# One turn per token tile in the first two tiles of a two-stage mixer, and a later split of one weight piece

## The chip, the cores and the metric

The kernel runs on one core of one Trainium2 chip. The metric is the device time of one execution in microseconds (us); less is better. Times of single instructions and waits come from one profiled execution.

## The reference

The input `x` is eight batches of 4096 tokens with 192 channels, in float32. A causal convolution of seven taps, with softmax-normalised weights per head, gives the tokens `x` of the mixer:

```python
u  = x + (relu(x.T @ w_tok1) @ w_tok2).T      # mixing over tokens, 4096 -> 256 -> 4096
out = u + relu(u @ w_ch1) @ w_ch2             # mixing over channels, 192 -> 1536 -> 192
```

The weights `w_tok1`, `w_tok2`, `w_ch1` and `w_ch2` come as 64-bit floats. The kernel reads their two 32-bit words and rebuilds a 32-bit float from them ("decoding").

## The kernel before

The batches are worked in groups: 0, 1, then three pairs. A group has eight tiles of 512 tokens. For each tile the kernel makes `u` (`mix2`: a product with `w_tok2` and an addition), turns it (TensorE transposes, so that channels lie on partitions), multiplies by `w_ch1` (`channel1`, six steps p = 0 to 5, each making two blocks of 128 of the 1536 columns, "a pair"), and by `w_ch2` (`channel2`). Most operands are held as a high part, rounded to the matmul's format, and a low part, which is the rest: ScalarE (ACT) copies the high part out of PSUM and VectorE (DVE) subtracts it. So `own_hi` and `own_lo` are the parts of the turned tokens, and `hh` and `hl` those of relu's result `h`. A step p of `channel1` is 18 matmuls on half the array's rows, two by two: high by high, low weight by high, and high weight by low, for three chunks of 64 channels (`channel1_mm`, L1220). Six PSUM buffers `ps_x` are shared by all of this.

Group 0's tile 0 is made while the weights are still being decoded: `stage1_first` writes out by hand the order of decoding, convolution and the hooks of tile 0 (L670 to L772). Tile 0 works without splitting `h`, with `first_channel2`; tile 1 is the first that runs through `channel1`. In these two tiles `u` is held twice, side by side (`doubled`, L1033; ACT copies the second one, L1093), and `transposed` (L1130) turns three chunks of 128 columns, each of them one chunk of 64 channels in both halves of the partitions. All later tiles of groups 0 and 1 use `transposed_once` (L1146): two chunks of 128 columns hold all 192 channels, and ACT then moves halves of them to the other half of the partitions for the third chunk: two moves for `own_hi` at once, and two for `own_lo` in the returned function (L1159 to L1161).

The instructions of each engine stand in the order in which the program writes them, and each engine works them off in that order. A planner (`Background`) decides where the work of the next group, the "background", is written between: it keeps two counters of planned time, `pe` and `dve`. `fg(pe, dve, after)` is called with every piece of the foreground and adds to both; `fill(after)` then writes background items as long as `dve` is less than `pe + after` (L105). The convolution of group 1 is such a background: its first item (`tap`, L938, and `taps`, L839) needs the first half of a block of `x` in the tile `raw0`, loaded by SyncE's queue (SP, L807), with a small GpSimd (POOL) memset on it (L809). Its gate is planned time, 10,000 counts after the load was written (L936), not the landing itself.

After tile 0, `first_channel2(..., transposed)` turns tile 1 in the midst of tile 0's last product (L1564). `second_split` (L777) ends the decoding of the last piece of `w_tok2` that is needed early (`t_second`) and splits it into `t2s`. The tiles `hh0`, `hl0` and so on of tile 1 lie in memory that tile 0 and the decoding used until then (`ht_ctx.close()`, L1572).

Of the kernel before, what the change touches and what calls it, by code (L numbers as in the profile page):

```python
# [142 lines left out]
def conv_mixer_kernel(ctx: ExitStack, tc: tile.TileContext, x, weight, w_tok1, w_tok2, w_ch1, w_ch2, out):  # L143
# [299 lines left out]
    def stage1_first(pe, p0, p1, pd, late, load_u, after, pieces, hooks):  # L443
# [308 lines left out]
        begin(N1 + 3)  # L752
        woven(chains[N1 + 2][1:])
# [22 lines left out]

        def second_split():  # L777
            woven(chains[LAST2 + 1][2:])
            woven(split(LAST2 + 1))

        return second, second_split
# [243 lines left out]
    def load_tile(gi, q, pool):  # L1025
# [7 lines left out]
        doubled = gi == 0 and q < 2  # L1033
        u = up.tile([P, TJ, ND, 2 if nb > 1 or doubled else 1, D2], F32, name="u", bufs=2)
        for i in range(nb):
            at = u[:, :, :, 1 if doubled else i]
# [18 lines left out]
    def mix2(gi, q, t2, u, at_once=False, turned=None, between=()):  # L1055
# [15 lines left out]
        for j in range(TJ):  # L1071
# [16 lines left out]
            one, two = uj[:, :, uj.shape[2] - 1], uj[:, :, 0]  # L1088
            if at_once:
                if j < len(between):  # L1090
                    between[j]()
                nc.vector.tensor_tensor(out=two, in0=rows(ps[:, :D]), in1=one, op=ALU.add)
                nc.scalar.copy(out=one, in_=two)  # L1093
            elif nb == 1:
                nc.vector.tensor_tensor(out=one, in0=rows(ps[:, :D]), in1=one, op=ALU.add)
                nc.vector.tensor_tensor(out=two, in0=rows(ps[:, D:2 * D]), in1=one, op=ALU.add)
# [32 lines left out]

    def transposed(u, between=()):  # L1130


        own = own_tile("hi"), own_tile("lo")
        for c in range(ND):
            ps = ps_x.tile([P, TT], F32, name="ps_x")
            for j in range(TJ):
                cols = u[:, j, c].rearrange("p b d -> p (b d)")
                nc.tensor.transpose(out=ps[:, j * P:(j + 1) * P], in_=cols, identity=ident)
            bg.fg(440, 600)
            nc.scalar.copy(out=own[0][:, c], in_=ps)  # L1140
            nc.vector.tensor_tensor(out=own[1][:, c], in0=ps, in1=f32(own[0][:, c]), op=ALU.subtract)
            if c < len(between):
                between[c]()
        return [(own, own)]
# [54 lines left out]
    def first_u(tokens_mm):  # L1199
        first["u"] = None, up.tile([P, TJ, ND, 2, D2], F32, name="u", bufs=2)  # L1200
# [4 lines left out]
        def out():  # L1205
            for k, ps in enumerate(pss):
                nc.scalar.copy(
                    out=first["u"][1][:, 2 * k:2 * k + 2, :, 1],
# [8 lines left out]
    def first_transposed(between=()):  # L1217
        first["abc"] = transposed(first["u"][1], between)

    def channel1_mm(t, p, order=((0, 0), (1, 0), (0, 1))):  # L1220
# [41 lines left out]
    def channel1(t):  # L1262
        h = {}
        for f0 in range(0, NF, NF // 3):
            for n in ("hh", "hl"):
                part = hp.tile([P, NF // 3, TT], F32R, name=f"{n}{f0}")
                for f in range(NF // 3):
                    h[n, order[f0 + f]] = part[:, f]
        bg.tiled = True
        for p in range(NP):  # L1270
            pss = channel1_mm(t, p)
# [86 lines left out]
    second, second_split = stage1_first(  # L1358
# [19 lines left out]
    sp = None  # L1378

# [72 lines left out]
    for gi, bs in enumerate(GROUPS):  # L1452
# [13 lines left out]
        for q in range(NT):  # L1466
            nxt = (gi, q + 1) if q + 1 < NT else (gi + 1, 0)
            for i, b in enumerate(bs):
# [19 lines left out]
                if ahead:  # L1488
                    h = channel1(abc[i])
# [62 lines left out]
                else:  # L1552
# [56 lines left out]
```

## Time and profile before

| what | value |
|---|---|
| median of 3 runs | 2010.44 us (2009.76 to 2010.59) |
| the profiled execution's own time | 2009.58 us |
| its span, first to last instruction | 2007.8 us |
| TensorE (PE) busy | 1999.8 us, 100% |
| VectorE (DVE) busy | 1506.9 us, 75% |
| ScalarE (ACT) busy | 785.6 us, 39% |
| chain that ended last | PE 93%, DVE 3%, DMA 2%, ACT 1% |

The span leaves out what lies around the first and last instruction, 1.78 us here. A matmul's end is modelled, so that rows of PE overlap; the pitch of their starts tells the rate. In rows of the timeline the bracket gives the engine's idle time before the instruction and what ended it.

### The profile page before, as it was taken

Reading aid. Unit: us, or ns where it says so; the run is one execution under the profiler, and the core shown is the slowest. Engines: PE = TensorE matmul, PEld = TensorE weight load, DVE = VectorE, ACT = ScalarE, POOL = GpSimd, SP = SyncE. Lnnn points to the kernel's source line nnn. Section 1 sums busy time; section 2 is a strip of 40 time slices with the busy share of each in tenths; the row PEclk is TensorE's granted clock in tenths of the full one; section 3 lists DMA queues with packets and bytes.
Section 4 is the critical chain, followed back from the end, with each engine's and each line's share of the span. In section 5 each row is a group of like instructions: output and inputs, shape, how many; then the busy total and the mean of one; then the engine's idle time right before and its main releaser. Section 6 shows DMA issues by size and latency. Waiting matters only on the chain.

```text
span 2007.8 us, 45323 instructions
## 1 busy us (share of the span) xinstructions
PE 1999.8 (100%) x19007; PEld 1860.0 (93%) x19007; DVE 1506.9 (75%) x3022; ACT 785.6 (39%) x1308; POOL 212.2 (11%) x375
## 2 busy tenths in 40 slices
PE   9999999999999999999999999999999999999999
PEld 9899999999999999999999999999999999999998
DVE  6899989999559999757888789556666666666664
ACT  6677544444343343323333433333233322333322
POOL 1000000000011101111101110111111110011110
PEclk9999999999999999999999999999999999999999
DMA  9946455553354567515346544533323222333310
GB/s 305 307 150 219 137 166 171 181 180 136 123 158 124 142 176 205 156 58 140 86 127 190 140 128 115 137 88 85 86 64 81 71 65 64 82 86 85 85 48 17
DMA packets 281792, 259.26 MB, mean 129 GB/s; under 512 B 190084, under 2 KB 231620, under 8 KB 281588
## 3 DMA queue, kind: packets, MB, share of 16 engines
q1 hardware_dynamic: 258404, 172.85, 30.7%
q0 software_dynamic: 22656, 83.12, 13.7%
q8 instruction: 150, 2.46, 0.5%
q14 instruction: 54, 0.44, 0.1%
q10 hardware_dynamic: 528, 0.39, 0.1%
HBM read 147.25 MB, written 71.30 MB: 109 GB/s over the span
## 4 chain that ended last, share of the span: by engine, by line
PE 93%; DVE 3%; DMA 2%; ACT 1%; SPq 0%; issue 0%; POOL 0%; ACTq 0%; POOLq 0%; DVEq 0%
PE ps_x L1231 38%; PE ps_x L1292 26%; PE ps_x L1311 11%; PE ps_x L1312 5%; PE ps_x L1110 3%; PE ps_a L925 2%; PE ps_a L926 2%; PE ps_a L927 2%; PE ps_x L1080 1%; PE ps_a L921 1%; PE ps_x L1083 1%; DMA dec_raw<-in_moe_w_tok_dram 1%; DVE xc L819 1%; PE ps_x L1085 1%; PE ps_x L1084 1%; PE ps_x L1154 1%
## 5 line engine op out<-in xcount | busy, mean ns | idle before, releaser
L1274 ACT ACTIVATE hh<-ps_x 128x512 fp32r<-128x512 f32 x756 | 410.5, 596 | 827.5 <-PE ps_x L1231 827.4
L1275 DVE SCALAR_TENSOR_TENSOR hl<-ps_x,hh 128x512 fp32r<-128x512 f32 x756 | 483.9, 683 | 173.5 <-ACT hh L1274 172.8
L1292 PE MATMUL ps_x<-w,hh 64*128 64x384 f32 x3648 | 523.4, 355 | 0.0
L1292 PE MATMUL ps_x<-w,hl 64*128 64x192 f32 x3648 | 462.0, 247 | 0.0
L1231 PE MATMUL ps_x<-other,w_hi 64*128 64x512 f32 x1728 | 448.0, 387 | 0.3 <-ACT other L1190 0.2
L819 DVE SCALAR_TENSOR_TENSOR xc<-raw,cw,xc 128x384 f32<-128x384 f32 (+1 forms) x768 | 388.4, 559 | 9.2 <-ACT xc L817 9.1
L1292 PEld LDWEIGHTS ps_x<-w,hl 64*128 64x128 f32 x3648 | 357.1, 188 | 1.7 <-DVE hl L1275 0.3
L1292 PEld LDWEIGHTS ps_x<-w,hh 64*128 64x128 f32 x3648 | 351.0, 184 | 1.4
L1231 PE MATMUL ps_x<-own_hi,w_hi 64*128 64x512 f32 x1440 | 348.4, 392 | 1.6 <-ACT own_hi L1140 0.5
L1311 PE MATMUL ps_x<-w,hh 128*128 128x384 f32 x1200 | 348.1, 361 | 0.0
L1231 PEld LDWEIGHTS ps_x<-other,w_hi 64*128 64x128 f32 x1728 | 315.2, 184 | 31.2 <-ACT other L1190 0.5
L1231 PE MATMUL ps_x<-own_hi,w_lo 64*128 64x512 f32 x1440 | 342.4, 387 | 0.0
L1231 PE MATMUL ps_x<-own_lo,w_hi 64*128 64x512 f32 x1440 | 342.3, 386 | 0.0
L1312 PE MATMUL ps_x<-w,hl 128*128 128x192 f32 x1200 | 300.4, 250 | 0.0
L1231 PEld LDWEIGHTS ps_x<-own_hi,w_hi 64*128 64x128 f32 x1440 | 214.6, 184 | 30.9 <-issue 4.3
L1231 PE MATMUL ps_x<-other,w_lo 64*128 64x512 f32 x864 | 242.0, 386 | 0.0
L1231 PEld LDWEIGHTS ps_x<-own_lo,w_hi 64*128 64x128 f32 x1440 | 219.3, 184 | 24.2
L1231 PEld LDWEIGHTS ps_x<-own_hi,w_lo 64*128 64x128 f32 x1440 | 219.1, 184 | 24.3
L1312 PEld LDWEIGHTS ps_x<-w,hl 128*128 128x128 f32 x1200 | 229.1, 191 | 0.0
L1311 PEld LDWEIGHTS ps_x<-w,hh 128*128 128x128 f32 x1200 | 225.3, 188 | 0.5 <-DVE hl L1275 0.4
L1300 DVE TENSOR_TENSOR osb<-ps_x,osb 128x192 f32<-128x192 f32 x456 | 163.0, 357 | 26.8 <-PE ps_x L1110 0.5
L1231 PEld LDWEIGHTS ps_x<-other,w_lo 64*128 64x128 f32 x864 | 159.0, 184 | 16.1
(187 smaller groups left out, 2022.7 us busy)
## 6 DMA issues: line engine op xcount, KB each, us to landing
raw<-in_x_dram SPq DMA_DIRECT2D x56, 672.0 KB, 7.6
t<-t2d SPq DMA_DIRECT2D x64, 512.0 KB, 5.5
out_dram<-osb POOLq DMA_DIRECT2D x62, 384.0 KB, 4.2
xcd<-xc POOLq DMA_DIRECT2D x28, 768.0 KB, 7.8
u<-xcd SPq DMA_DIRECT2D x56, 384.0 KB, 5.7
t<-t1p SPq DMA_DIRECT2D x32, 512.0 KB, 5.8
other<-own_hi POOLq DMA_DIRECT2D x24, 384.0 KB, 3.9
other<-own_lo POOLq DMA_DIRECT2D x24, 384.0 KB, 4.0
```

The lines of the kernel that those rows point to most:

```text
L819: nc.vector.scalar_tensor_tensor(out=dst, in0=src, scalar=cw[:, h, k:k + 1], in1=dst, op0=ALU.mult, op1=ALU.add)
L925: nc.tensor.matmul(out=ps, lhsT=wh, rhs=xh, start=a, stop=False)
L926: nc.tensor.matmul(out=ps, lhsT=wh, rhs=xl, start=False, stop=False)
L927: nc.tensor.matmul(out=ps, lhsT=wl, rhs=xh, start=False, stop=z)
L1110: nc.tensor.matmul(out=ps[:, :n], lhsT=t2[ks, kc, r, j, :], rhs=h1[ks, kc, v, :n], start=m == 0, stop=m == len(prods) - 1)
L1231: nc.tensor.matmul(out=ps, lhsT=w1[w][rows, chunks[h][c], p * P:(p + 1) * P], rhs=t[h][v][rows, c], start=n == 0, stop=n == len(prods) - 1,)
L1274: nc.scalar.activation(out=h["hh", f], in_=ps, func=AF.Relu)
L1275: nc.vector.scalar_tensor_tensor(out=h["hl", f], in0=ps, scalar=0.0, in1=f32(h["hh", f]), op0=ALU.max, op1=ALU.subtract)
L1292: nc.tensor.matmul(out=ps[:, :m], lhsT=h[part, f][ks, ts], rhs=w2[ks, f, :m], start=n == 0 and part == "hh", stop=z and part == "hl",)
L1300: nc.vector.tensor_tensor(out=osb[:, j], in0=v, in1=osb[:, j], op=ALU.add)
L1311: nc.tensor.matmul(out=ps[:, :2 * D], lhsT=h["hh", f][:, ts], rhs=w2[:, f, :], start=n == 0, stop=False)
L1312: nc.tensor.matmul(out=ps[:, :D], lhsT=h["hl", f][:, ts], rhs=w2[:, f, :D], start=False, stop=z)
```

## The change

- **Tokens turned once.** `transposed` and `doubled` go; tiles 0 and 1 use `transposed_once`, with `u` held once. ACT no longer copies `u`. Tile 0's two moves of `own_lo` (`first["rest"]`) stand behind the start of the next decoding; tile 1's stand right behind `first_channel2`.
- **Order of the products.** Only in step p = 0 are the products of the third chunk put last; the other steps take chunk after chunk.
- **First parts of h in idle memory.** In tile 1, `channel1` puts `hh` and `hl` of the first two steps into the tiles `stage` and `xc1` of the background's pools (`early_parts`), all but the second low part.
- **The last piece of `w_tok2`.** Its decoding ends before tile 1's `channel1` (`second_end`); it is split (`second_split`) behind the second pair's `hh`.
- **Planner.** The extra counts on `dve` are 4000 and then 2000 in place of 6000, and the stores of `w_tok2` may begin after tile 1 in place of tile 0.

```diff
+        first["rest"]()                         # stage1_first, behind begin(N1 + 3)
...
+        def second_end():
+            woven(chains[LAST2 + 1][2:])
+
         def second_split():
-            woven(chains[LAST2 + 1][2:])
             woven(split(LAST2 + 1))
+            bg.dve = max(bg.dve, bg.pe) + 2e3
...
-        doubled = gi == 0 and q < 2
-        u = up.tile([P, TJ, ND, 2 if nb > 1 or doubled else 1, D2], F32, name="u", bufs=2)
+        u = up.tile([P, TJ, ND, nb, D2], F32, name="u", bufs=2)
...
-                nc.vector.tensor_tensor(out=two, in0=rows(ps[:, :D]), in1=one, op=ALU.add)
-                nc.scalar.copy(out=one, in_=two)
+                nc.vector.tensor_tensor(out=one, in0=rows(ps[:, :D]), in1=one, op=ALU.add)
...
+        if len(t) > 2 and not p:
             prods = [(w, v, c) for cs in (range(ND - 1), [ND - 1]) for w, v in order for c in cs]
...
+    def early_parts():
+        high, low = (td.tile([P, 2 * TT], F32R, name="stage", bufs=2).rearrange("p (f t) -> p f t", t=TT) for _ in range(2))
+        more = sp0.tile([P, NF // 4, TT], F32R, name="xc1")
+        return ("hh", 0, high), ("hl", 0, low), ("hh", 2, more)
...
             for f, ps in pss:
                 nc.scalar.activation(out=h["hh", f], in_=ps, func=AF.Relu)
+            if early and p == 1:
+                between()
+                part("hl", 0, range(2, 4))
+            for f, ps in pss:
...
-                    h = channel1(abc[i])
+                    h = channel1(abc[i], second_split, early_parts if gi == 0 and q == 1 else None)
...
-                        first_channel2(u, osb, [3], (NF // 3, lambda: made.extend(transposed(loaded[1]))))
-                        abc = made
-                        second_split()
-                        first["parted"] = 0.0
-                        bg.dve = max(bg.dve, bg.pe) + 6e3
+                        first_channel2(u, osb, [3], (NF // 3, lambda: made.extend(transposed_once(loaded[1]))))
+                        abc, rest = made
+                        rest()
+                        second_end()
+                        bg.dve = max(bg.dve, bg.pe) + 4e3
...
+                if gi == 0 and q == 1:
+                    first["parted"] = 0.0
```

The order of the instructions on ACT, from the turning of tile 1 to its first relu results; `own_hi` and `own_lo` are tile 1's turned tokens, `xc` is the convolution of group 1, `raw` its input, `hh` relu's high part. Before:

```order
L1140 CAST own_hi<-ps_x 128x512 x3
L240 CAST t2s<-t_second 128x2x512
L1325 DMA out_dram<-osb 128x4x192
L1274 ACTIVATE hh_929<-ps_x 128x512 x4
L1274 ACTIVATE hh_931<-ps_x 128x512 x4
L1274 ACTIVATE hh_933<-ps_x 128x512 x2
L199 ACTIVATE dec_top<-dec_raw 128x512
L817 ACTIVATE xc_1077<-raw_787,cw 128x8x24 x2
```

And with the change (its lines are numbered anew: L1142 is the copy of `own_hi`, L1146 and L1147 are the moves, L821 the first tap, L1269 relu, L1324 the store):

```order
L1142 CAST own_hi<-ps_x 128x512 x2
L1146 CAST own_hi<-own_hi 64x512
L1147 CAST own_hi<-own_hi 64x512
L821 ACTIVATE xc_896<-raw_780,cw 128x8x24 x2
L1146 CAST own_lo<-own_lo 64x512
L1147 CAST own_lo<-own_lo 64x512
L1324 DMA out_dram<-osb 128x4x192
L1269 ACTIVATE stage<-ps_x 128x512 x2
L1269 ACTIVATE xc_919<-ps_x 128x512 x2
L240 CAST t2s<-t_second 128x2x512
```

The first two taps of the convolution moved from behind ten relu copies to a place ahead of tile 1's moves of `own_lo`.

The matmuls of tile 1's step p = 0 on PE, behind the turning, and the first rows of p = 1, with the change; before, p = 0 had the form in which p = 1 stands here:

```order
L1140 MATMUL ps_x<-ident,u 128x128 x8
L1237 MATMUL ps_x<-w2f,t2s 128x192
L1237 MATMUL ps_x<-w2f,h_last 128x192 x3
L1218 MATMUL ps_x<-own_hi,w_hi 128x512 x4
L1218 MATMUL ps_x<-own_hi,w_lo 128x512 x4
L1218 MATMUL ps_x<-own_lo,w_hi 128x512 x4
L1218 MATMUL ps_x<-own_hi,w_hi 128x512 x2
L1218 MATMUL ps_x<-own_hi,w_lo 128x512 x2
L1218 MATMUL ps_x<-own_lo,w_hi 128x512 x2
L1218 MATMUL ps_x<-own_hi,w_hi 128x512 x6
```

The last two matmuls of p = 0 read the third chunk of `own_lo`, which ACT's two moves make. The turning is 8 transposes in place of 12.

The loads around `raw` on SP's queue, with the change; before, the same loads stood in the same order:

```order
L538 DMA xcd_75<-kept_x_119 90x8x192
L538 DMA xcd_75<-kept_x_119 32x8x192
L262 DMA dec_raw<-in_moe_w_tok_dram 128x1024 x2
L811 DMA raw_780<-in_x_dram 128x14x96
L811 DMA raw_783<-in_x_dram 128x14x96
L874 DMA t_786<-t1d 128x512
```

Nothing moved there: `raw_780`, which the first tap reads, is the third load after the stores `xcd` as before.

## Rows read from the trace of the kernel before

**Rows 1.** The page's chain that ended last, by engine.
```profile
PE 93%; DVE 3%; DMA 2%; ACT 1%; SPq 0%; issue 0%; POOL 0%; ACTq 0%; POOLq 0%; DVEq 0%
```

**Rows 2.** Waits of PE over the whole span: us in total, times, longest us.
```profile
PE ps_x L612 <- POOL ident masks.py:199: 1.4, 1, 1.4
```

**Rows 3.** Timeline of PE, tile 1: start us, us, engine, line, what.
```profile
87.32 1.47 PE L1138 MATMUL ps_x<-ident,u 128*128 128x128 f32 x12
88.63 0.49 PE L1250 MATMUL ps_x<-w2f,t2s 128*128 128x192 f32 x2
...
90.03 0.96 PE L1231 MATMUL ps_x<-own_hi,w_hi 64*128 64x512 f32 x6
...
94.92 0.84 PE L1231 MATMUL ps_x<-own_hi,w_lo 64*128 64x512 f32 x6
95.60 0.84 PE L1231 MATMUL ps_x<-own_lo,w_hi 64*128 64x512 f32 x6
96.67 1.56 PE L1231 MATMUL ps_x<-own_hi,w_hi 64*128 64x512 f32 x6 [0.23 <-DVE hl L1275]
...
102.62 1.06 PE L1231 MATMUL ps_x<-own_lo,w_hi 64*128 64x512 f32 x6
```

**Rows 4.** Timeline of ACT, the same stretch.
```profile
87.96 1.56 ACT L1140 CAST own_hi<-ps_x 128x512 fp32r<-128x512 f32 x3 [1.22 <-PE ps_x L1138]
93.71 1.05 ACT L240 CAST t2s<-t_second 128x1024 fp32r<-128x1024 f32 x1 [4.19 <-DVE t_second L208]
93.73 0.46 ACTq L1325 DMA_DIRECT2D out_dram<-osb  x1
94.66 3.03 ACT L1274 ACTIVATE hh<-ps_x 128x512 fp32r<-128x512 f32 x6
...
102.99 0.79 ACT L817 ACTIVATE xc<-raw,cw 128x192 f32<-128x192 f32 x2
```

**Rows 5.** Timeline of SP's queue: issues of DMAs.
```profile
70.01 4.19 SPq L1043 DMA_DIRECT2D u<-xcd  x4
...
88.76 1.65 SPq L262 DMA_DIRECT2D dec_raw<-in_moe_w_tok_dram  x2
90.51 3.28 SPq L807 DMA_DIRECT2D raw<-in_x_dram  x2
...
101.23 1.80 SPq L1043 DMA_DIRECT2D u<-xcd  x4
```

**Rows 6.** Instructions on the tile `raw`, 85 to 112 us: issue to landing.
```profile
DMA to landing us min/median/max: 8.3/9.6/11.0
```

**Rows 7.** Timeline of POOL, the memset on `raw`'s first half.
```profile
99.19 0.57 POOL L809 MEMSET raw<- 1x576 f32 x1 [87.19 <-DVE hl L1275]
```

**Rows 8.** Line L1160, a move of `own_lo`: ns min/median/max, first and last start.
```profile
L1160 ACT CAST own_lo<-own_lo x14: 617/619/622, 119.6 to 547.0; 64x512 fp32r<-64x512 f32 x14
```

**Rows 9.** Windows: length, PE, PEld, DVE, ACT, POOL busy, PEclk, DMA share, GB/s.
```profile
72.00:77.00 5.00, 4.50 (x27) 4.06 (x26) 4.83 (x8) 3.50 (x5) 0.00 (x0) 1.00 0.87 222
82.00:90.00 8.00, 8.00 (x54) 7.78 (x52) 7.09 (x14) 4.04 (x8) 0.00 (x0) 1.00 1.00 314
```

**Rows 10.** Line L612 at the kernel's start: the timeline, and two windows.
```profile
1.37 8.72 PE L612 MATMUL ps_x<-ident 128*128 128x128 f32 x54 [1.37 <-POOL ident masks.py:199]
...
3.00:5.00 2.00, 2.00 (x11) 2.00 (x10) 1.00 0.78 243
7.00:9.00 2.00, 2.00 (x21) 2.00 (x20) 1.00 1.11 345
```

**Rows 11.** Windows at the span's end, the columns of rows 9.
```profile
2004.00:2006.00 2.00, 0.42 (x4) 0.19 (x2) 0.72 (x2) 0.00 (x0) 0.00 (x0) 1.00 0.00 0
2006.00:2008.00 2.00, 0.00 (x0) 0.00 (x0) 0.00 (x0) 0.00 (x0) 0.00 (x0) 0.74 0.15 49
```

**Rows 12.** Timeline of PE, tile 2's step p = 1, in the order by chunks.
```profile
122.77 0.62 PE L1231 MATMUL ps_x<-own_hi,w_hi 64*128 64x512 f32 x4
123.22 0.62 PE L1231 MATMUL ps_x<-own_hi,w_lo 64*128 64x512 f32 x4
```

More of the change, by code (lines that the diff above doesn't have):

```diff
@@ L775, in second @@
             woven(chains[LAST2 + 1][:2])
+        def second_end():
+            woven(chains[LAST2 + 1][2:])
         def second_split():
-            woven(chains[LAST2 + 1][2:])
             woven(split(LAST2 + 1))
-        return second, second_split
+            bg.dve = max(bg.dve, bg.pe) + 2e3
+        return second, second_end, second_split
     def stage1(gi, pools):
@@ L1032, in load_tile @@
                 nc.sync.dma_start(out=f32(t2[:, kc]), in_=t2d[q2][:, kc, :, h * TJ:(h + 1) * TJ, :])
-        doubled = gi == 0 and q < 2
-        u = up.tile([P, TJ, ND, 2 if nb > 1 or doubled else 1, D2], F32, name="u", bufs=2)
+        u = up.tile([P, TJ, ND, nb, D2], F32, name="u", bufs=2)
         for i in range(nb):
-            at = u[:, :, :, 1 if doubled else i]
+            at = u[:, :, :, i]
             if gi:
@@ L1087, in mix2 @@
             uj = u[:, j]
-            one, two = uj[:, :, uj.shape[2] - 1], uj[:, :, 0]
+            one = uj[:, :, 0]
             if at_once:
@@ L1091, in mix2 @@
                     between[j]()
-                nc.vector.tensor_tensor(out=two, in0=rows(ps[:, :D]), in1=one, op=ALU.add)
-                nc.scalar.copy(out=one, in_=two)
+                nc.vector.tensor_tensor(out=one, in0=rows(ps[:, :D]), in1=one, op=ALU.add)
             elif nb == 1:
                 nc.vector.tensor_tensor(out=one, in0=rows(ps[:, :D]), in1=one, op=ALU.add)
-                nc.vector.tensor_tensor(out=two, in0=rows(ps[:, D:2 * D]), in1=one, op=ALU.add)
+                nc.vector.tensor_tensor(out=one, in0=rows(ps[:, D:2 * D]), in1=one, op=ALU.add)
             else:
@@ L1128, in own_tile @@
         return up.tile([P, ND, TT], F32R, name=f"own_{n}")
[L1130 to L1144, printed above, removed]
     def transposed_once(u):
@@ L1199, in first_u @@
     def first_u(tokens_mm):
-        first["u"] = None, up.tile([P, TJ, ND, 2, D2], F32, name="u", bufs=2)
+        first["u"] = None, up.tile([P, TJ, ND, 1, D2], F32, name="u", bufs=2)
         pss = [ps_x.tile([P, TT], F32, name="ps_x") for _ in range(2)]
@@ L1207, in out @@
                 nc.scalar.copy(
-                    out=first["u"][1][:, 2 * k:2 * k + 2, :, 1],
+                    out=first["u"][1][:, 2 * k:2 * k + 2, :, 0],
                     in_=ps[:, :2 * D].rearrange("p (j c d) -> p j c d", j=2, d=D2),
@@ L1215, in first_mix, with first_transposed @@
         mix2(0, 0, *first["u"], at_once=True, between=between)
-    def first_transposed(between=()):
-        first["abc"] = transposed(first["u"][1], between)
+    def first_transposed():
+        first["abc"], first["rest"] = transposed_once(first["u"][1])
     def channel1_mm(t, p, order=((0, 0), (1, 0), (0, 1))):
@@ L1260, in conv_mixer_kernel, with channel1, part @@
     order = [p + h * NP for p in range(NP) for h in range(2)]
-    def channel1(t):
+    def channel1(t, between=None, early=None):
         h = {}
[L1264 to L1268, printed above, removed]
+        def part(n, p, fs=range(NF // 3)):
+            made = hp.tile([P, NF // 3, TT], F32R, name=f"{n}{2 * p}")
+            for f in fs:
+                h[n, order[2 * p + f]] = made[:, f]
         bg.tiled = True
         for p in range(NP):
-            pss = channel1_mm(t, p)
+            if early and not p:
+                for n, k, v in early():
+                    for f in range(2):
+                        h[n, order[k + f]] = v[:, f]
+            elif p % 2 == 0:
+                part("hh", p)
+                part("hl", p)
+            pss = list(channel1_mm(t, p))
             bg.fg(2040 if p else 2400, 1300)
@@ L1357, in conv_mixer_kernel @@
     pieces = [range(0, 1), range(1, 2), range(2, 4), range(4, 6)]
-    second, second_split = stage1_first(
+    second, second_end, second_split = stage1_first(
         pe, p0, p1, pd, first_late, first_u, first_done, pieces,
```

## The prediction

> **What bounds the kernel now.** I read the chain that ended last first: 93% of it is PE [rows 1]. The list of PE's waits over the whole span comes next; its longest entry is the 1.4 us at the start [rows 2], and no later one is longer. So nothing downstream has slack that could take up a delay: what PE loses in the first tiles, the kernel loses. Then I read the stretch that the change rewrites, tile 1's turning and `channel1`, engine by engine. On PE the reader is to see an even pitch (18 matmuls of a pair take three times 0.68 us, so 2.04 us) with one hole: the matmuls that start at 95.60 are six of the third pair, and the next start only at 96.67 [rows 3], since all six PSUM buffers are full. The hole's cause is on ACT: it sat idle for 4.19 us before the cast of `t_second` and copied the first relu results only at 94.66 [rows 4], though PE had ended the first pair some 2.5 us before. This row also shows that ACT keeps its written order: work that was ready stood behind a wait.
>
> **Part 1: the turning.** Tiles 0 and 1 lose four transposes each. Twelve take 88.63 - 87.32 = 1.31 us, 0.11 us each [rows 3], so 0.44 us a tile. Tile 1's first pair could then start at 90.03 - 0.44 = 89.6 us. The copies of `u` and a third of the `own_lo` subtractions go too; ACT and DVE are not the bound there. Four moves a tile come in, 0.62 us each on ACT [rows 8]; those of `own_hi` lie beside the first 12 matmuls. All savings in tile 0 and up to 89.6 us, and any delay of tile 0 by its own moves, which are at most 4 x 0.62 = 2.5 us, fall in front of the wait of part 2 and are swallowed by it: I count them at nothing.
>
> **Part 2: the tap ahead of the moves.** This is the term that matters. The printed order has the convolution's first two taps on ACT between the moves of `own_hi` and those of `own_lo`. The cause is the planner: with three chunks turned, its `dve` counter stood at 35,040 against a `pe` of 34,800, more than the 200 allowed; with two chunks it stands at 34,000 against 33,920, which lets the taps through. Their gate is planned time only. On the chip the load of `raw` is issued at 90.51 [rows 5] and lands at the soonest 8.3 us later [rows 6], at 98.8; the memset on it runs from 99.19 to 99.76 [rows 7]. ACT comes to the taps when its copies and moves of `own_hi` are done: it starts copying at 87.96 [rows 4], two of three copies are 1.04 us, two moves 1.24, so about 90.3. It then waits for some 9.5 us, and behind it stand the moves of `own_lo`, the store of tile 0 and all relu copies. DVE is held as well, since its own taps stand behind `own_lo`.
>
> PE gets on with 16 of the 18 matmuls of the first pair, at 0.68 / 6 = 0.113 us each: from 89.6 to 91.4. The last two need the moved third chunk of `own_lo`. That is ready 0.79 us (two taps [rows 4]) + 1.24 us (two moves) + about 0.2 us of handing over after the memset, so at 99.76 + 2.2 = 102.0, or 3.2 us after the landing. PE then has two matmuls, 0.23 us, and five pairs, 10.2 us: `channel1` ends at 112.4. Before, its last six matmuls started at 102.62 and end, by the pitch, at 103.3 [rows 3]. **The difference is 9.1 us.** It already holds the gain of the old hole.
>
> **Part 3: does the load land sooner?** SP's order around it is the same. But tile 1's `u` now comes in pieces of 768 bytes in place of 256: its four issues took 4.19 us, and those of tile 2, which had the wider pieces, 1.80 us [rows 5]. Tile 0's store, issued at 93.73 before [rows 4], no longer runs beside the load. Against this, the DMA engines were busy from 82 to 90 us (share 1.00) and only a little idle before (0.87 in 72 to 77) [rows 9], so that SP's lead is mostly spent in the queue. Bounds: nothing, and 2.4 + 1.2 us (the store's 0.39 MB at 314 GB/s), 3.6 us. I take the idle share, 0.13 x 5 = 0.65 us, half of the store, 0.6 us, and a little for the smaller number of pieces: **1.5 us sooner**. The Trainium skill, "DMA: Bandwidth & Descriptors", Specifications, says that a transfer in pieces under 512 bytes falls short of the full rate because it is read, modified and written. If that meant a second pass over `u`'s 0.39 MB, another 1.2 us would come off, and the sum below would be 9.0 in place of 10.2 us. The rows speak for less: 222 GB/s at a share of 0.87 is 255 GB/s while busy, against 314, with other transfers between.
>
> **Part 4: the clock.** PE then idles from 91.4 to about 100.5 us. At the span's end TensorE's granted clock fell: the last matmuls stand in 2004 to 2006, and the mean of 2006 to 2008 is 0.74 [rows 11], so it went from 2.4 to 1.2 GHz about half way through, some 2.5 us after the last matmul. So I expect 1.2 GHz when PE goes on. What that costs until it rises is bounded by nothing and by the kernel's start: there the same transposes run at 11 in 2 us and later at 21 in 2 us (the column of the granted clock shows 1.00 for both; the pitch shows the two levels), and 54 of them took 8.65 us in place of 54 x 0.11 = 5.9 [rows 10]. **I take all of this, 2.6 us**, as the nearest row, also because a slower PE hides the backlog on DVE.
>
> **Part 5: what costs nothing.** The new order in steps p = 1 to 5: four matmuls by chunks have a pitch of 0.45 us [rows 12], 0.113 us each, the same as six in the old order of tile 1. The early parts of `h` and the later split take away the hole at 96.67, which the sum has already. After the wait, relu copies, DVE's decoding of `t_second` and its split come in a row; with six PSUM buffers PE may meet a hole of some tenths at the fifth pair, 0 to 0.5 us, which I put at nothing while PE is slow.
>
> **The sum**: 9.1 - 1.5 + 2.6 = 10.2 us on the profiled execution's 2009.58 us gives 2019.8. That execution is 0.86 us below the median of the runs shown; on the median, 2010.44, it is **2020.6 us**.
>
> **Rivals.**
> - *The wait is hidden, no slower than before.* If ACT finds the load landed, the change gains the hole (13.27 us for six pairs in place of 12.24, so 1.0 us) and the transposes of both tiles, 0.9 us: 2008.5 us. This needs PE to go on by 103.3 - 10.4 = 92.9, a landing by 89.7 us, which lies before the load's issue at 90.51. For it speaks only that SP may run 2.4 us ahead; against it that the DMA engines had no idle share there. Chance 0.07.
> - *The clock holds, or comes back at once.* Then only 9.1 - 1.5 = 7.6 us: 2018.0 us. Against it stands the fall at the span's end, after a shorter idle time. Chance 0.14.
> - *Nothing lands sooner, and the backlog bites*: 9.1 + 2.7 + 0.5 = 12.3 us, 2022.7 us. For it speaks the full share of the DMA engines. Chance 0.17.
> - The forecast: 0.62.
>
> **How the numbers follow.** A measurement of this kernel can tell about 0.2%, 4.0 us, from no change. Forecast and the second and third rival are all slower by over that, 0.93; I keep 0.02 of it back for a load that comes much earlier than I can see. The first rival is within 0.2%, except for a small part with gains that I have not seen, 0.02. So faster 0.02, same 0.07, slower 0.91. The forecast's own bounds are 2018.5 (a landing 3.6 us sooner) to 2022.1; the range takes in the second and third rival, from 2016.9 to 2023.0.
>
> **What would show it.** In the profile after, ACT should sit idle from about 90.3 to 98 or 100 us before the first `xc`, with the memset of `raw` as the releaser; PE should have one gap of 8 to 10 us inside tile 1's first pair, ended by the move of `own_lo`; the granted clock should read below 1.00 around 95 to 105 us; and the rest of the kernel should be the old one, shifted. `raw` should land at about 97.3. The prediction is wrong if ACT passes the taps without a wait, if PE's gap is under 4 us, or if a delay at 105 us is smaller at the end.

## The result, and the profile after

| | before | with the change |
|---|---|---|
| median, runs side by side | 2010.72 us (2009.76 to 2011.48, 6 runs) | **2026.62 us** (2024.47 to 2028.37, 6 runs) |
| ratio to before | | 1.0080, 95% interval 1.0069 to 1.0090 |
| the profiled execution's own time | 2009.58 us | 2025.05 us |
| its span | 2007.8 us | 2023.2 us |

The kernel is slower by 15.9 us on the medians, 15.4 us on the spans. The forecast was slower by 10.2 us, 2020.6 us, with a range from 2016.9 to 2023.0: the direction was right, and the size lies outside.

The page of the profile after: the span, the busy time by engine, and the chain that ended last, by engine.

```profile
span 2023.2 us, 45294 instructions
...
PE 2002.1 (99%) x18999; PEld 1855.2 (92%) x18999; DVE 1506.3 (74%) x3020; ACT 787.9 (39%) x1306; POOL 212.2 (10%) x375
...
PE 88%; DVE 7%; DMA 3%; ACT 1%; issue 1%; SPq 1%; POOL 0%; POOLq 0%; DVEq 0%; ACTq 0%
```

PE's busy time is only 2.3 us longer, so most of the loss is waiting. In [rows 1] PE held 93% of the chain, now 88%; DVE's share has grown from 3% to 7%, DMA's from 2% to 3%. PE's waits over the whole span (total, times, longest) say where:

```profile
PE ps_x L1218 <- ACT own_lo L1147: 10.3, 2, 8.8
PE ps_x L1218 <- DVE hl L1274: 2.5, 3, 1.7
PE ps_x L612 <- POOL ident masks.py:199: 1.4, 1, 1.4
PE ps_x L1218 <- ACT own_hi L1142: 1.3, 1, 1.3
```

Against [rows 2], whose longest entry was the 1.4 us at the start, there are two longer ones: 8.8 us for the moves of `own_lo`, which was forecast, and 1.7 us for `hl`, which was not. First the forecast one. ACT in tile 1's turning, the answer to [rows 4]:

```profile
89.49 1.08 ACT L1142 CAST own_hi<-ps_x 128x512 fp32r<-128x512 f32 x2 [6.49 <-PE ps_x L1140]
90.59 0.62 ACT L1146 CAST own_hi<-own_hi 64x512 fp32r<-64x512 f32 x1
91.23 0.62 ACT L1147 CAST own_hi<-own_hi 64x512 fp32r<-64x512 f32 x1
99.85 0.80 ACT L821 ACTIVATE xc<-raw,cw 128x192 f32<-128x192 f32 x2 [8.00 <-POOL raw L813]
100.68 0.62 ACT L1146 CAST own_lo<-own_lo 64x512 fp32r<-64x512 f32 x1
101.32 0.62 ACT L1147 CAST own_lo<-own_lo 64x512 fp32r<-64x512 f32 x1
```

ACT stands still for 8.00 us in front of the taps, ended by the memset on `raw`; the two moves come behind. PE in the same stretch (the answer to [rows 3]):

```profile
92.84 0.39 PE L1218 MATMUL ps_x<-own_hi,w_lo 64*128 64x512 f32 x2
101.99 0.80 PE L1218 MATMUL ps_x<-own_lo,w_hi 64*128 64x512 f32 x2 [8.76 <-ACT own_lo L1147]
102.58 1.48 PE L1218 MATMUL ps_x<-own_hi,w_hi 64*128 64x512 f32 x6
103.86 1.45 PE L1218 MATMUL ps_x<-own_hi,w_lo 64*128 64x512 f32 x6
105.14 0.86 PE L1218 MATMUL ps_x<-own_lo,w_hi 64*128 64x512 f32 x6
...
110.12 1.56 PE L1218 MATMUL ps_x<-own_hi,w_hi 64*128 64x512 f32 x6
111.30 1.07 PE L1218 MATMUL ps_x<-own_hi,w_lo 64*128 64x512 f32 x6
...
115.04 0.44 PE L1083 MATMUL ps_x<-h,t2s 128*128 128x384 f32 x1
```

PE goes on at 101.99. The groups of six at 102.58 and 103.86 take 1.28 us each by their starts, the later ones 0.68: this is the lower of the clock's two levels, 1.2 GHz (granted clock 0.50). At 110.12 six take 1.18 us, a hole of the form that [rows 3] has at 96.67. The row at 115.04 is the first matmul of `channel2`. The last matmul of tile 1's `channel1` starts at 114.72; before it was 103.30. So 11.4 us are lost by there, and some 4 us must come later. Comparing the end of `channel1` tile by tile, tile 2 is 11.6 us later and tile 3 16.1; then it stays between 15.0 and 15.4 to the end. In tile 3 ACT shows the same form of wait at another place. First before, where both decoding copies (`dec_top`, L199) are done ahead of tile 3's relu copies (`hh`):

```profile
151.15 0.67 ACT L199 ACTIVATE dec_top<-dec_raw 128x512 f32<-128x512 f32 x1
152.07 0.62 ACT L240 CAST t2s<-dec_top 128x512 fp32r<-128x512 f32 x1 [0.26 <-DVE dec_top L208]
152.60 1.08 ACT L1274 ACTIVATE hh<-ps_x 128x512 fp32r<-128x512 f32 x2
```

With the change:

```profile
166.25 1.07 ACT L1269 ACTIVATE hh<-ps_x 128x512 fp32r<-128x512 f32 x2
167.22 1.22 ACT L1439 CAST stage<-t2s 128x512 fp32r<-128x512 f32 x1
171.73 0.66 ACT L199 ACTIVATE dec_top<-dec_raw 128x512 f32<-128x512 f32 x1 [3.29 <-DMA dec_raw<-in_moe_w_tok_dram]
172.29 1.07 ACT L1269 ACTIVATE hh<-ps_x 128x512 fp32r<-128x512 f32 x2
```

SP's queue, which issues that load:

```profile
163.95 0.35 SPq L262 DMA_DIRECT2D dec_raw<-in_moe_w_tok_dram  x1
```

And PE behind it:

```profile
170.93 1.07 PE L1218 MATMUL ps_x<-own_lo,w_hi 64*128 64x512 f32 x6
173.66 1.56 PE L1218 MATMUL ps_x<-own_hi,w_hi 64*128 64x512 f32 x6 [1.66 <-DVE hl L1274]
```

A decoding copy waits for a piece of `w_tok2` that was issued at 163.95, and starts 7.8 us after that issue; tile 3's next relu copies stand behind it on ACT until 172.29; PE fills its PSUM buffers and stops. Tile 3's `channel1` takes 15.2 us (163.0 to 178.2) in place of 12.2. This I call the second hole. It is 3.1 of the 4.4 us that are added between the ends of tiles 2 and 3. The other 1.3 us lie ahead of tile 3's `channel1` and are given back: the stretch behind it is 1.3 us shorter than before (21.2 in place of 22.5 us), and experiment 5, which has no such hole, shows the same shift.

### The profile page after: what moved, and what is told of

Read it like the earlier page. It is cut to its first block, busy times and chain, and to the rows that moved or that the text cites. A ratio compares the mean times of both kernels' runs of the same rounds, so it can differ in the third digit from the quotient of the medians.

```text
span 2023.2 us, 45294 instructions
## 1 busy us (share of the span) xinstructions
PE 2002.1 (99%) x18999; PEld 1855.2 (92%) x18999; DVE 1506.3 (74%) x3020; ACT 787.9 (39%) x1306; POOL 212.2 (10%) x375
## 4 chain that ended last, share of the span: by engine, by line
PE 88%; DVE 7%; DMA 3%; ACT 1%; issue 1%; SPq 1%; POOL 0%; POOLq 0%; DVEq 0%; ACTq 0%
PE ps_x L1218 36%; PE ps_x L1291 25%; PE ps_x L1310 10%; PE ps_x L1311 5%; PE ps_x L1112 3%; DVE xc L823 3%; PE ps_a L929 2%; PE ps_a L930 2%; PE ps_a L931 2%; PE ps_x L1083 1%; DVE hl L1274 1%; DMA dec_raw<-in_moe_w_tok_dram 1%; DMA raw<-in_x_dram 1%; DMA x<-in_x_dram 1%; PE ps_x L1086 1%; PE ps_x L1088 1%
## 5 line engine op out<-in xcount | busy, mean ns | idle before, releaser
L1269 ACT ACTIVATE hh<-ps_x 128x512 fp32r<-128x512 f32 x752 | 408.5, 596 | 834.7 <-PE ps_x L1218 834.6
L1291 PEld LDWEIGHTS ps_x<-w,hl 64*128 64x128 f32 x3648 | 350.9, 188 | 1.9 <-DVE hl L1274 0.5
L1291 PEld LDWEIGHTS ps_x<-w,hh 64*128 64x128 f32 x3648 | 345.5, 184 | 1.5
L1310 PE MATMUL ps_x<-w,hh 128*128 128x384 f32 x1184 | 342.3, 360 | 0.2 <-DVE hl L1274 0.2
L1218 PE MATMUL ps_x<-own_hi,w_hi 64*128 64x512 f32 x1440 | 336.7, 393 | 4.2 <-DVE hl L1274 2.5
L1218 PE MATMUL ps_x<-own_lo,w_hi 64*128 64x512 f32 x1440 | 330.4, 387 | 10.3 <-ACT own_lo L1147 10.3
L1218 PE MATMUL ps_x<-own_hi,w_lo 64*128 64x512 f32 x1440 | 330.5, 388 | 0.0
L1218 PEld LDWEIGHTS ps_x<-other,w_lo 64*128 64x128 f32 x864 | 159.2, 184 | 16.8
```

The lines of the kernel that those rows point to most:

```text
L1218: nc.tensor.matmul(out=ps, lhsT=w1[w][rows, chunks[h][c], p * P:(p + 1) * P], rhs=t[h][v][rows, c], start=n == 0, stop=n == len(prods) - 1,)
L1291: nc.tensor.matmul(out=ps[:, :m], lhsT=h[part, f][ks, ts], rhs=w2[ks, f, :m], start=n == 0 and part == "hh", stop=z and part == "hl",)
L1310: nc.tensor.matmul(out=ps[:, :2 * D], lhsT=h["hh", f][:, ts], rhs=w2[:, f, :], start=n == 0, stop=False)
```

## The experiments

Medians differ by a few us between kernels here, and several of them vary by 4 to 6 us from run to run, so the profiled execution is used for where, the medians for how much.

**1. The taps later.** The changed kernel; only the gate of group 1's first taps differs.

```diff
-            return at if nb > 1 else at + (4e3 if q2 else 10e3)
+            return at if nb > 1 else at + (4e3 if q2 else 20e3)
```

> The changed kernel with one number altered: the planned-time gate of group 1's first taps is 20,000 counts after the load in place of 10,000, so that ACT has them behind eight of tile 1's relu copies and no longer ahead of the moves of own_lo. Theory A (the wait of these taps for raw on ACT makes the delay of tile 1; a second hole of PE of some 3 us in tile 3, where ACT waits for dec_raw ahead of relu copies, has its own cause in the planner's order): no gap of PE over 1 us in tile 1, its channel1's last matmul starts at 103.3 to 104.3 us in place of 114.7, and since ACT's order in tile 3 is still that of the changed kernel, the second hole of 2 to 3.5 us stays: 2013 to 2015.5 us. Rival B (the moves themselves, or the borrowed memory of the first parts of h, hold PE up): a gap of 5 us or more stays in tile 1, 2018 us or more. Rival C (the second hole only follows from the first): both go, 2009.5 to 2011.5 us.

Measured: 2014.57 us (2013.75 to 2017.91), ratio 1.0025 (1.0015 to 1.0035), 4.5 us over the 2010.12 of before. Tile 1's `channel1` ends at 104.2, without a gap over 1 us. The second hole stayed, and the profiled execution, the slowest of the eight, shows a long one. ACT, then PE:

```profile
156.72 1.21 ACT L1439 CAST stage<-t2s 128x512 fp32r<-128x512 f32 x1
162.38 0.66 ACT L199 ACTIVATE dec_top<-dec_raw 128x512 f32<-128x512 f32 x1 [4.45 <-DMA dec_raw<-in_moe_w_tok_dram]
```

```profile
160.41 1.08 PE L1218 MATMUL ps_x<-own_lo,w_hi 64*128 64x512 f32 x6
164.30 2.25 PE L1218 MATMUL ps_x<-own_hi,w_hi 64*128 64x512 f32 x6 [2.81 <-DVE hl L1274]
165.92 1.91 PE L1218 MATMUL ps_x<-own_hi,w_lo 64*128 64x512 f32 x6
```

Theory A holds; B falls (the moves and the borrowed memory are all still there), and so does C: the second hole does not come from the first. Here PE goes on at half clock too after its idle time of 2.81 us (granted clock 0.50 from 164 to 170 us, six matmuls in 1.28 us from 165.92), and tile 3's `channel1` takes 19.0 us.

**2. The taps early in the kernel before.** Nothing of the change but the place of the taps.

```diff
-            bg.fg(440, 600)
+            bg.fg(440, 600, 500)
```

(in `transposed`, L1130; the third number is `after`)

> The kernel before with one number altered: in the turning of three chunks the planner may go 500 counts ahead in place of 200, so that ACT has group 1's first two taps ahead of the copy of tile 1's third chunk. Nothing else of the change is in it. Theory A (the taps' wait for raw is the cost): ACT idles from about 90 to 99.8 us ahead of the taps, PE's first matmuls of tile 1's channel1 come at 101.5 to 102.5 us in place of 91, its last one starts at 113 to 115, and the time is 2020 to 2024 us. Rival B (the cost comes with the single turning, the moves or the borrowed memory): no gap over 2 us in tile 1, 2009.5 to 2012 us.

Measured: 2022.65 us (2018.69 to 2024.02), ratio 1.0058 (1.0046 to 1.0071), 12.5 us over before. ACT, then PE:

```profile
87.89 1.56 ACT L1140 CAST own_hi<-ps_x 128x512 fp32r<-128x512 f32 x3 [1.23 <-PE ps_x L1138]
98.65 0.80 ACT L817 ACTIVATE xc<-raw,cw 128x192 f32<-128x192 f32 x2 [9.20 <-POOL raw L809]
```

```profile
94.17 0.39 PE L1231 MATMUL ps_x<-own_hi,w_hi 64*128 64x512 f32 x1
100.22 1.64 PE L1231 MATMUL ps_x<-own_hi,w_hi 64*128 64x512 f32 x5 [5.67 <-DVE osb L1258]
```

The cost comes with the taps alone; B falls a second time. What the edit does I had wrong. Where a call names no `after` it is 600 (L111), so 500 is less, not more: each call leaves `dve` 100 counts lower. At the next call, that of `first_channel2` with the 200 (L1254), `dve` then stands 140 counts over `pe` in place of the prediction's 240, and the taps pass. So they stand behind the third chunk's copy and not ahead of it, and PE got through two pairs before it stopped, where I had its gap ahead of the first. Its last matmul starts at 113.6, within what was expected, but by other delays: after the wait ACT stood a further 3.22 us for DVE's decoding of `t_second`, and the granted clock was 0.50 up to 108 us.

**3. The moves ahead of the taps.** In tile 1 (`whole`) the planner is called only once all copies and moves are written.

```diff
-            bg.fg(440, 600)
+            if not whole:
+                bg.fg(440, 600)
             nc.scalar.copy(out=own[0][:, c], in_=ps)
...
         moved(0)
+        if whole:
+            moved(1)
+            for c in range(ND - 1):
+                bg.fg(440, 600)
```

> The changed kernel with tile 1's moves of own_lo written ahead of the taps; the taps still stand ahead of the relu copies. Theory A (ACT's written order is all that matters, and raw lands at 98 to 99.8 us whatever stands around it): PE fills its six PSUM buffers with three pairs, until about 97, then waits 3 to 5 us until the taps are done (about 100.7) and the first relu copies have run; the last matmul of tile 1's channel1 starts at 107 to 109 in place of 114.7, and the time is 5 to 8 us below the changed kernel's: 2018.5 to 2021.5 us. Rival B (the moves or the borrowed memory hold PE up): PE still stops in the first pair, no more than 2 us are gained. Rival D (raw lands later or sooner by some us when PE and ACT go on): the gap's length differs from 3 to 5 us, and raw's memset shows it.

Measured: 2023.21 us (2020.98 to 2026.07), ratio 1.0067 (1.0053 to 1.0081), 3.4 us below the changed kernel's median where 5 to 8 were expected; the interval overlaps with the changed kernel's. The moves no longer hold PE up in its first pair, so B falls. But PE gets through two pairs and one matmul, not the three pairs expected: it stops, as in experiment 2, until DVE's addition into `osb`, which reads a `ps_x` buffer of tile 0's last product.

```profile
94.70 0.39 PE L1224 MATMUL ps_x<-own_hi,w_hi 64*128 64x512 f32 x1
100.46 1.64 PE L1224 MATMUL ps_x<-own_hi,w_hi 64*128 64x512 f32 x5 [5.38 <-DVE osb L1251]
```

That is 17 matmuls, 1.9 us, less done ahead of the gap, and the gap is over the 3 to 5 us expected. I had also left the half clock out of my own expectation, and here PE works at it for longer, from 100.5 to about 105.5 us. Tile 1's `channel1` ends at 110.9, not 107 to 109. The second hole stays too: tile 3's `channel1` takes 16.8 us.

**4. Transposes in the wait.** The changed kernel with PE kept at work; the transposes are added work and go into a buffer that nothing reads. They stand behind the 12th matmul of the pair, not the 16th as I wrote ahead of the run.

```diff
+            if n == 6 and len(t) > 2 and not p and first.pop("busy", None):
+                for k in range(72):
+                    nc.tensor.transpose(
+                        out=first["acc"][:, k % TJ * P:(k % TJ + 1) * P], in_=ident, identity=ident
+                    )
```

> The changed kernel with 72 transposes of the identity, 0.11 us each, put on PE between the 16th and the 17th matmul of tile 1's first pair, into a PSUM buffer that nothing uses yet: PE works through most of its 8.8 us of waiting. Theory A (of the 11.4 us in tile 1, about 1.3 are the half clock with which PE goes on from 102 to 105 us; transposes keep the clock up, as the 54 transposes at the kernel's start brought it up): granted clock 0.95 or more from 95 to 105 us, PE goes on at 102.0, no group of six matmuls takes over 0.75 us, and the time is 1 to 1.5 us below the changed kernel's. Rival E (transposes don't keep the clock up, or other work such as the decoding on DVE sets the pace behind the wait anyway): half clock after the wait as before, or full clock with PE waiting for PSUM instead; the time is that of the changed kernel within 0.5 us. By the Trainium skill, TensorE: Matmul & The Clock Gate, Part 4, transposes don't count as busy for the clock; that would be rival E.

Measured: 2026.54 us (2022.18 to 2028.18), by the median no gain. The stretch itself says more. Busy time of each engine by windows and the granted clock (the third number from the end), of the changed kernel:

```profile
100.00:102.00 2.00, 0.01 (x2) 0.01 (x2) 1.66 (x4) 1.89 (x4) 0.57 (x1) 0.50 1.04 359
102.00:104.00 2.00, 2.00 (x10) 1.63 (x12) 1.97 (x3) 1.08 (x2) 0.00 (x1) 0.50 1.02 318
104.00:106.00 2.00, 2.00 (x16) 1.58 (x14) 0.96 (x2) 0.00 (x0) 0.00 (x0) 0.71 0.80 269
```

and of the kernel with the transposes:

```profile
100.00:102.00 2.00, 1.60 (x12) 0.93 (x12) 1.97 (x5) 1.39 (x3) 0.57 (x1) 1.00 0.80 210
102.00:104.00 2.00, 2.00 (x22) 1.62 (x20) 2.00 (x3) 1.02 (x3) 0.00 (x0) 1.00 0.87 249
104.00:106.00 2.00, 2.00 (x22) 1.65 (x20) 0.25 (x1) 1.97 (x4) 0.00 (x0) 1.00 1.01 341
```

PE's resume and the first matmul of `channel2`, with the transposes:

```profile
101.28 0.50 PE L1224 MATMUL ps_x<-own_lo,w_hi 64*128 64x512 f32 x2 [0.40 <-ACT own_lo L1148]
...
112.87 0.44 PE L1084 MATMUL ps_x<-h,t2s 128*128 128x384 f32 x1
```

From the wait's end to the first matmul of `channel2` PE needs 11.59 us (101.28 to 112.87), against 13.05 (101.99 to 115.04): between these two executions the half clock costs **1.46 us**, as theory A has it. In the whole time of the profiled execution tile 3 gave it back: its `channel1` took 19.1 us, 15.2 in that of the changed kernel, as ACT waited 4.54 us for `dec_raw` in place of 3.29 and the granted clock was 0.50 from 174 to 178 us. The single executions differ in the same way. Two of the five, with a mean granted clock of 1.000 and 0.999 over the whole span, took 2022.18 and 2022.38 us, over 2 us less than any of the changed kernel's six; the other three, at 0.997 and 0.998, took 2026.54 to 2028.18. The Trainium skill, "TensorE: Matmul & The Clock Gate", Part 4, says that transposes don't count as busy for the clock; this run shows otherwise for these 72 in float32, with 1.00 from 95 us on and none of PE's other work between 92.1 and 100.1.

**5. Taps later and no decoding in `channel1`.** To the first experiment's gate comes a gate on ACT's first decoding copy; `bg.tiled` is set while `channel1`, or `channel2` with all PSUM buffers, is written.

```diff
-                add(0, 22e3 if i == 0 and not loaded else 0, fn, eager=loaded and i == 0)
+                add(0, 22e3 if i == 0 and not loaded else 0, fn, gate=lambda: None if bg.tiled else 0.0, eager=loaded and i == 0)
```

> The run with the later tap gate, and one more edit: the planner may not begin a decoding piece (ACT's first copy out of dec_raw) while channel1 or channel2 of a tile is written with all PSUM buffers, so that no such copy stands between tile 3's relu copies. Theory A (the second hole is ACT waiting for dec_raw's landing with relu copies behind it): tile 1's channel1 ends at 104.2 as in that run, tile 3's takes 12.2 to 12.7 us with no gap of PE over 1 us, and the time is that of the kernel before plus the 0.9 to 1.3 us by which tile 0 is later: 2010.8 to 2012 us. Rival F (the load or the piece is late anyway, and the wait only moves to another place, to the relu copies or the mix of tile 4): a hole of 2 us or more in tile 3, 4 or 5, 2012.5 to 2016 us.

Measured: 2010.47 us (2010.07 to 2011.48), ratio 1.0003 (0.9995 to 1.0012), 0.6 us over the 2009.83 of before and a little under what was expected. No gap over 1 us in tiles 1 to 5; tile 1 ends at 104.8, a little behind the expected 104.2 of experiment 1: in this execution tile 0's `channel1` already began 0.7 us later than there. Tile 3's takes 12.7 us. Theory A; F falls. With both waits away, all the rest of the change costs next to nothing and gains nothing.

**6. No decoding in `channel1` alone**, the taps left where the change put them (only the last diff).

> The changed kernel with that second edit alone; the taps wait as in the changed kernel. Theory A: tile 1's channel1 ends at 114 to 115, no gap over 1 us in tile 3, and from there on everything is 10.8 to 12 us later than in the kernel before: 2021 to 2022.5 us, with a narrower spread of the times than the changed kernel's, since the wait for dec_raw depends on how the transfers fall. Rival F (the wait moves): 2024 us or more. What is then left over the kernel before is the price of the taps' wait, clock and backlog included.

Measured: 2019.97 us (2019.22 to 2022.89), ratio 1.0055 (1.0042 to 1.0067), 10.1 us over before; a little under what was expected. The `hl` wait is gone from PE's list, and only the first is left:

```profile
PE ps_x L1218 <- ACT own_lo L1147: 9.6, 2, 8.9
```

The spread, 3.7 us, is hardly narrower than the changed kernel's 3.9, so that part of the expectation fell. The profiled execution, 2022.27 us, lies 2.3 us over the median, and its granted clock was low twice: 0.63 and 0.68 from 55 to 65 us, where tile 0's `channel1` took 16.2 us in place of the changed kernel's 14.4, and 0.50 from 98 to 106 us. From the resume at 103.09 to `channel2` it needed 13.64 us, 2.05 more than the 11.59 of experiment 4.

**7. The stores later, in the kernel before.** One of the planner's numbers alone, everything else as before.

```diff
-                        first["parted"] = 0.0
...
+                if gi == 0 and q == 1:
+                    first["parted"] = 0.0
```

> The kernel before with one part of the change alone: the stores of w_tok2 may begin after tile 1 in place of tile 0. The turning, the taps, the parts of h and the split are the old ones. By the printed order ACT's decoding copies then stand in tile 3 as in the changed kernel (one ahead of the relu copies, the next behind the first two). Theory A2 (this part alone makes the second hole): tile 1's channel1 ends at 103.3 as before, PE has a gap of 2 to 5 us in tile 3's channel1 ended by a relu copy or hl, and the time is 2012.5 to 2017 us. Rival G (the hole needs the delay of tile 1 or the other counts on the planner): no gap over 1 us in tile 3, 2009.5 to 2011 us.

Measured: 2016.08 us (2014.51 to 2016.48), ratio 1.0030 (1.0018 to 1.0041), 6.2 us over before. Tile 1 ends at 103.4 as before; in tile 3 ACT shows the changed kernel's picture:

```profile
155.69 1.19 ACT L1435 CAST stage<-t2s 128x512 fp32r<-128x512 f32 x1
160.30 0.66 ACT L199 ACTIVATE dec_top<-dec_raw 128x512 f32<-128x512 f32 x1 [3.42 <-DMA dec_raw<-in_moe_w_tok_dram]
```

Theory A2; G falls. This edit alone makes the second hole. In the kernel before, tile 3's two decoding copies both stood ahead of its relu copies; now the second stands behind the first two. By which of the planner's shares the later stores move the decoding I did not follow further.

**8. Tile 0 turned as before**, on top of experiment 5: tile 0 by `transposed` with doubled `u`, tile 1 by `transposed_once`. The line that chooses:

```diff
-        first["abc"], first["rest"] = transposed_once(first["u"][1])
+        first["abc"], first["rest"] = transposed(first["u"][1], between), lambda: None
```

> The kernel with the later tap gate and no decoding in channel1, and with tile 0 turned in three chunks as before (its u doubled, no moves), so that only tile 1 is turned once. Theory A (tile 0's single turning costs 0.9 to 1.3 us, since PE waits for the moves of own_hi and own_lo some 1.9 us more than before and saves four transposes, 0.44 us; tile 1's saves its four transposes and the hole at the third pair): tile 1's channel1 starts at 89.4 to 89.8 and ends at 102 to 103.3, and the time is 0.3 to 1.2 us below the kernel before: 2009 to 2010 us. Rival H (tile 0's delay has no part in it, because tile 1 is held by ACT or the decoding of w_tok2 anyway): tile 1's channel1 ends at 103.8 to 104.3, and the time is that of the run with those two edits alone.

Measured: 2010.49 us (2008.82 to 2013.55), ratio 1.0003 (0.9994 to 1.0012): not told apart from before or from experiment 5. The profiled execution is the slowest, and shows a cost that I had put at nothing:

```profile
97.29 1.09 ACT L1287 ACTIVATE stage<-ps_x 128x512 fp32r<-128x512 f32 x2 [3.89 <-DMA xcd<-kept_x]
```

The "idle" memory of the first parts of `h` is `stage`, whose place `kept_x` had before; when its store runs late, relu's first copy waits for it. It had also lost time by then: tile 0's `channel1` began at 57.15, before at 55.38, with a granted clock of 0.50 from 12 to 14 us. So the run decides nothing between A and H.

**9. The first part in `xc1`**, on top of experiment 8.

```diff
-        return ("hh", 0, high), ("hl", 0, low), ("hh", 2, more)
+        return ("hh", 0, more), ("hl", 0, low), ("hh", 2, high)
```

> The kernel with tile 0 turned as before, the later tap gate and no decoding in channel1, with one exchange: relu's first high part goes to xc1 and the second pair's to stage, not the other way round. In the profiled run of that kernel relu's first copy waited 3.9 us for the store of kept_x, whose memory stage takes over; xc1 has no such wait. Theory A3 (this wait, which comes and goes from run to run, spreads the times of that kernel from 2008.8 to 2013.6 us): relu's first copy starts right behind PE's first pair, tile 1's channel1 ends at 102 to 103.3, the times lie within 1.5 us of each other and their median is 2008.8 to 2009.7 us, 0.1 to 1.2 us below the kernel before. Rival I (the spread comes from the start of the kernel, before 57 us, or from the transfers in tile 3): the spread stays 3 us or more and the median at 2010 to 2011 us.

Measured: 2009.75 us (2008.72 to 2012.33), ratio 0.9995 (0.9986 to 1.0004), beside 2010.88 for before. Relu's first copy no longer waits for a DMA, but the spread stayed 3.6 us, and tile 1 ended at 103.5: the median fits theory A3 nearly, the spread rival I, for which the late start in experiment 8's profile also speaks. Undecided.

**10. The whole change, mended.** Experiment 5 with that exchange, and tile 0's moves of `own_lo` directly behind those of `own_hi` (the line that did this later goes).

```diff
-        first["abc"], first["rest"] = transposed_once(first["u"][1])
+        first["abc"], rest = transposed_once(first["u"][1])
+        rest()
```

> All of the change (both tiles turned once), with the later tap gate, no decoding in channel1, the first high part of h in xc1, and tile 0's moves of own_lo directly behind those of own_hi, ahead of the decoding's copy. Theory A: PE's wait for tile 0's own_lo falls from 1.9 to 0.5 to 1.2 us, tile 0's channel1 ends 0.5 to 1.2 us sooner than in the run with the gate and no decoding, and the time is 2009.5 to 2010.3 us, within 0.03% of the kernel before. Rival J (the decoding that is held up for 1.2 us on ACT costs PE the same later, in tile 0's channel2 or at tile 1's start): 2010.3 to 2011.5 us, no better than that run.

Measured: 2010.00 us (2008.70 to 2012.14), ratio 0.9997 (0.9988 to 1.0006). PE's wait for tile 0's `own_lo` fell from 1.50 us in the changed kernel to 0.55:

```profile
58.34 0.50 PE L1218 MATMUL ps_x<-own_lo,w_hi 64*128 64x512 f32 x2 [0.55 <-ACT own_lo L1146]
```

and tile 1's `channel1` ends at 102.6 in the profiled execution, 0.7 us sooner than before. The median lies in theory A's range, but by the time of the whole kernel it cannot be told from before. No version here beats the kernel before by more than the measurement can tell.

The two causes side by side, medians over the kernel before measured beside each:

| kernel | taps wait for `raw` | decoding copy among tile 3's relu copies | us over before |
|---|---|---|---|
| the change | yes | yes | 15.9 |
| 6 | yes | no | 10.1 |
| 2 (kernel before, taps alone) | yes | no | 12.5 |
| 1 | no | yes | 4.5 |
| 7 (kernel before, stores alone) | no | yes | 6.2 |
| 5 | no | no | 0.6 |

From experiment 5 the two add up to 0.6 + 9.5 + 3.9 = 14.0 us, from the kernel before to 12.5 + 6.2 = 18.7; the change lies between. Whether the two waits lengthen or shorten each other was not tried, and the executions of one kernel differ by as much as these sums do.

## Why the prediction was right about the first wait and missed the second

The step that failed is part 5 with the sign that goes with it, "the rest of the kernel should be the old one, shifted": the sum ends with tile 1, and nothing was put down for what the planner writes behind it. There the runs showed a second wait, of 3.9 to 6.2 us. Up to there three terms were wrong, and their errors partly cancel: 10.2 + 1.5 (part 3) - 1.1 (part 4) + 0.7 (part 5's backlog) = 11.3 us, where 11.4 was measured at the end of tile 1; 15.4 was measured at the end of the span.

- **What bounds the kernel**: held. What PE lost in the first tiles came out at the end: 11.4 us at the end of tile 1, and with tile 3's hole 15.4.
- **Part 1, the turning, nothing**: held for the time, though nothing was saved up to there. Tile 0 was in fact delayed: PE waited 1.32 us for `own_hi` and 1.50 us for `own_lo`, and tile 1 began at 91.1, where 89.6 was forecast and 90.0 stood before. The wait of part 2 swallowed it.
- **Part 2, the taps, 9.1 us**: held. The resume was put at 102.0 when nothing lands sooner, and it was 101.99, with the memset at 99.25 in place of 99.19. Experiments 1 and 2 show the cause from both sides.
- **Part 3, 1.5 us sooner**: fell, for this pair of profiles; `raw` did not land at about 97.3. From its issue to its memset it took 8.27 us in place of 8.68, but the issue came at 90.98, 0.47 us later. SP's four issues of `u` took 3.2 us in place of 4.2, but they began 1.05 us later. Over the profiles, the memset came 7.8 to 8.5 us after the issue in the five kernels in which tile 0's store stands behind the waiting taps, and 8.7 to 10.6 (mean 9.6) in the seven in which it runs beside the load. That fits a share of the store of some 1.4 us, more than the 0.6 I took; but the store alone was not moved, and the profile of before, from which I worked, was the best of the seven. The width of `u`'s pieces shows no effect: 7.94 us with 256 bytes (experiment 2), 8.48 with 768 (experiment 4). The sentence on the Trainium skill's "DMA: Bandwidth & Descriptors", Specifications, would have made the sum 9.0 us; no row here shows that gain.
- **Part 4, the clock, 2.6 us** (its own numbers, 8.65 - 5.9, give 2.7): right in kind, too large for this execution. Half clock came, and cost 1.46 us against experiment 4's profile. But the price differs from one execution to the next: experiment 6, with tile 1 written alike, paid 2.05 us, as the clock stayed low until about 107.5 us (0.61 in the window from 106 to 108), some 4.5 us behind its resume in place of 3.2. And the profiled execution of the changed kernel has the highest mean granted clock of its six, 0.998; the others show 0.997 and 0.996. What the clock cost the median is not shown.
- **Part 5, nothing**: this is the step that failed. The backlog's hole was bounded by 0.5 us and was about 0.7 (1.18 in place of 0.68 us for six, and 0.2 before it); a slower PE did not cause it, since experiment 4 has it at full clock. Within tile 1 the parts then are 9.1 + 1.5 (the clock) + 0.7 = 11.3 us. The rest is what this part did not price at all: the later stores of `w_tok2`, named in the section on the change and left out of the sum. They moved a decoding copy in between tile 3's relu copies, where it waits for a load: 3.9 to 6.2 us by experiments 1, 5 and 7. I had read the printed order only around tile 1, though the planner carries every altered count on through the whole group.
- **The rivals**: the hidden wait and the holding clock did not come. "Nothing lands sooner, and the backlog bites" named two true things and lay 3.9 us under the result for the same reason as the forecast. With the second hole taken away (experiment 6) the time is 2019.97 us, inside the range, but with the help of errors that partly cancel, and not because each term was right.

## What to carry to other kernels

When a planner with counters writes the order, an edit of one count has to be read through to the end of everything that the planner still places, not only at the edited place: here the second wait came two tiles later, and with the same shape as the first. Each time ACT, which keeps its written order, was given a copy that waits for a load, ahead of work that PE needs: the moves of `own_lo`, then the relu copies that free PSUM. So go through the printed order of such an engine, and ask of every instruction that reads a loaded tile what stands behind it. A gate in planned time says nothing about the landing. And read the default of a call before altering its argument: in experiment 2 the edit went the other way than I thought.

## What the runs showed that I had not expected

How a hole of PE goes on behind its end differs from run to run. In the changed kernel's tile 3 PE went on at full clock after an idle time of 1.66 us; in the first experiment's, after 2.81 us, at half clock. In experiment 7 the idle time was 1.76 us and PE went on at full clock, but the granted clock was down to 0.50 in the window from 164 to 166 us, when PE was at work again. So a wait on ACT for one load could cost PE more than its own length, and that cost differed from run to run: tile 3's `channel1` took 15.2, 16.8, 17.0, 19.0 and 19.1 us in five profiles with the second hole, against 12.2 before, and the mean granted clock over it was 1.00, 0.90, 0.90, 0.82 and 0.82. The times of whole executions go the same way, in experiment 4 above and in the changed kernel: 2025.05 us at a mean granted clock of 0.998, 2024.47 and 2026.03 at 0.997, 2027.22 to 2028.37 at 0.996. That goes with the spread of these kernels; that it makes most of it was not tested.
